# The key weights' request waits for GpSimd's constants, and the order of all engines is laid out anew

## The chip, the cores and the metric

The kernel runs on one core of a Trainium2 chip. Its engines are TensorE (PE; its weight loads are listed as PEld), VectorE (DVE), ScalarE (ACT), GpSimd (POOL) and SyncE (SP). The metric is device time in microseconds (us), the median of the runs.

## The reference

Four layers stand one behind the other on a sequence of 2048 rows of 512 numbers (bf16), and each is added to its input. Layers 1 and 3 are linear attention with 32 heads of 16 numbers, layers 2 and 4 are attention in a sliding window of 256 rows. Both kinds use one set of weights each.

```python
def _A_ref(x, wqkv, wo):                       # linear attention
    q, k, v = ...                              # x @ wqkv, by heads
    phi = lambda t: jnp.where(t > 0, t + 1, jnp.exp(t)) + 1e-6
    pq, pk = phi(q), phi(k)
    kv = jnp.einsum("bhsd,bhse->bhde", pk, v)  # sums over all rows
    z = jnp.einsum("bhsd->bhd", pk)
    num = jnp.einsum("bhqd,bhde->bhqe", pq, kv)
    den = jnp.einsum("bhqd,bhd->bhq", pq, z)[..., None] + 1e-6
    return ... num / den ... @ wo

def _B_ref(x, wqkv, wo):                       # window of W = 256 rows
    scores = jnp.einsum("bhqd,bhkd->bhqk", q, k) * (Dh ** -0.5)
    p = _softmax(jnp.where(mask, scores, -1e9))
    return ... p @ v ... @ wo

x = A_x
x = x + _A_ref(_layernorm(x), A_wqkv, A_wo)
x = x + _B_ref(_layernorm(x), B_wqkv, B_wo)
x = x + _A_ref(_layernorm(x), A_wqkv, A_wo)
x = x + _B_ref(_layernorm(x), B_wqkv, B_wo)
```

## The kernel before

The rows are cut into 16 tiles of 128, which stay in SBUF as `xres` from the first load to the last store. A tile passes through these steps. DVE takes mean and variance (line 811, 812), GpSimd the reciprocal root (814), DVE writes the normalized rows `xn` (817). They are transposed, by PE with a copy by ACT (832 and 842) for the first tiles of a layer and by a DMA that SP issues (825) for the others. PE multiplies them with the weights: line 855 makes rows by features (keys, values and the output product in the linear layers), line 867 features by rows. In a linear layer ACT takes exponentials and positive parts (876, 879), DVE joins them into `pk` or `pq` (877, 880), line 913 sums keys times values over all tiles into one PSUM bank, and line 1228 (`kvz`) closes the sums; only then can any tile's output follow (935, 944 to 947). So the first layer needs all 16 tiles' keys and values before its first output. In a window layer the scores (1004, 1052) go through ACT's exponentials (1031, 1073; 304 of them, the bulk of ACT's work), are masked by DVE (1039, 1091) and multiplied with values (1107, 1123).

Every step is recorded as a numbered operation with its engine, what it reads and what it writes. `ORDER` is a list of these numbers that a search outside of the kernel wrote: it sets in which order each engine issues its operations, which PSUM banks they take (the numbers after a colon), and which of two engines does an operation (a mark behind the number). `schedule` follows the list and only adds the waits; it moves nothing. The durations and the `land` times that stand beside operations are the search's estimates; on the chip they have no effect.

The start. GpSimd writes small constants (lines 722 to 730); DVE clears `zero` and makes the identity matrix, and later some masks. PE multiplies zeros (1265, "warm"), then branches out of that code. Each engine's first part is laid out ahead of a slow general version of the kernel, so each engine branches over that once; the operation `jump` (`warm` on PE) marks where. `loads()` issues the transfers, one behind the other on each queue: SP tile 0, 1 and 2, the value weights `w_Av`, tile 3, its branch, tile 4, the query weights `w_Aq`, and the rest; ACT the key weights `w_Ak` alone, behind its table load. ACT also fills buffers that later steps only write in part: ones in `vA` and `vt` (692), zeros in `vbd` (695, two halves), which the first window layer needs. Because `graph()` gives `deps[...] = None` for operations on one engine, that edge is an order without a wait; `True` makes a wait on a semaphore.

Of the kernel before, what the change touches and what calls it, by code (L numbers as in the profile page):

```python
# [13 lines left out]
D = 512  # L14
# [321 lines left out]
292 276:4.3.0 296:0.3 185 283 277 235 213 225:7.0 219:5.0.1 280 278 237 293 295 240 236 284' 18 19 21 279 281 220 221 262:4.4.3 263 223 222 224 238 241 264  # L336
248:6.5.0 297 266 298' 265 249 252 250 191:3.6.1 226 192 254:5.4 227' 255 195 193 197:4.5 198 256' 194 267 196 268:3.6 269 199 242 270 251 60 253 299 300:0
# [13 lines left out]
917:1 650 651 933 966 664' 1390 452 683:7.1.0 938:0.5.5 684 929 690 1387:4.0 967 473 1388 939 937 940 685' 1389' 969:0.2.1 1391 686 687 942:7 474:5.2 475 1392  # L351
943 944 970 476 661 941 971 945:0 477 946:2 947:4 1026:0.2.0 1027 1028 478:3 465:7 466 961:5.0.0 962 963 691:1 706 948 949 467 950:1 951 675:7.1 1000:2.5.2
1001 1002 994 676 677':1 964 918:4 919 973:0.2.3 920 707 1403 479:2 1404 678 680:7.3 681 1030 952:3 480:6 481 974 975 1004:0.4.5 977:3 482 982:2 682 1405
1393:3 665:7.0.1 666 953:6 2671 1406:0 972 679 954 1005 1006 976 968 692:2 667 955 724 1416 1007 1061:0.4.1 978 1062 1063 725 983 984 985:3 996:0.6.0 997 998
979 980:0 981:1 986 1407:1 693:5.2 694 1035:0.3.1 1036 708 726 701:2.2.4 1003 668 695':2 742 727:2 1417 1408:7.0.1 1409 709:1 1037 1008:0.5.3 702 698:4.0 699
# [5 lines left out]
492 493:2 1105:4.6.4 729:2.4 730 1106 1082:3 1107 731':1 1077 732 1135 1078:0.4.5 1083 734:2.2 722 740 1079 1084 1080 1109:0.6.1 1110 1111 735 1023:5 1085:1  # L361
# [4 lines left out]
765:3.0 775' 516 1092:0 1448:5 1461:7 1143 766 518 770:2.0 1134 767':0 1176 1177 1148:0.6.1 771 755:5.1.1 772' 509:1 768 769 1139 1093:4 1094 1149 1150 1095  # L366
1179:0.2.3 1157:7 1152:6 1205 1204 1180 1181 756 757 510:4 511 1147 1236:0.2.0 1151 1153 776 512 1470 528:5.15.1 529 778 1158 1154 1237 1238 532 1171:0.2.0
530 1169 779 1182 1155:0 531 1159 1160:3 1156:3 1161 1172 1127:2 780 758 1162:3 1467:4.3 1468 1210:0.5.5 1173 1211 1212 1462:7.3.3 1463 1128:3 1178 781:3
782:2 1170 1469' 759 1174 1240 777 1646:2.16.2 1213 1464 1465 1129 1130 1466 1183:0.4.2 1187:6 1188 1189 1184 1185 1190:2 1647 519:0.1 520 1191:1 1650 521 522
533 1163:3 1214:4.6.1 1648 523:2 1215 1216 1164 791:2.0.0 792 524:0 1206:0.4.0 1165 1649 1498 1499 1192:3 793 534:6.0 1186 1207 535 536 1193 537 538:0 1208  # L370
1471 1449:2.4.0 1450 1472 1239 1209 1500 1451 1194 1195:3 1245:0.6.4 783:5.1 784 1452 539:1 1196 1453 1473:1 1246 1501:0 1247 788:4.1 789 785:1 790'
1218:0.2.3 1474:6 794 525:7 526 1219 1220 786 787 1222:6 1271:0.4.1 1272 527 796 1651 1223 797 540:7 798 1224 1273 1502:15 1485 1217 799:2 1486 795 1487
# [67 lines left out]
class _Kernel:  # L440
# [816 lines left out]
    def graph(self):  # L1257
# [23 lines left out]
        for o in s.ops:  # L1281
            if o.name.startswith("fill") and "ACT" in o.engs:
                o.deps[table] = None
# [100 lines left out]
```

## Time and profile before

| | |
|---|---|
| median of three runs | 410.61 us (409.73 to 410.74) |
| profiled execution, its own time | 411.51 us |
| its span, first to last instruction | 410.1 us |
| mean granted TensorE clock | 0.996 |
| busy: PE, ACT, DVE, POOL | 386.0, 374.0, 369.2, 106.0 us |

The profile is of one execution, so its durations are held against 411.51 us. In a row of the timeline stand the start and the length in us, the engine (SPq and ACTq are what a queue issues), the line, the operation, output<-input, how many, and in brackets how long the engine had been idle before and what ended that. In rows by stretches stand the stretch, its length, and for each engine the busy time and the instructions that began in it, then the granted clock (1.00 is full), the mean busy share of the DMA engines and GB/s. Matmuls overlap in the pipeline: each is listed with its whole length, but the next begins after some 0.2 us.

### The profile page before, as it was taken

How to read it: one execution, taken by the hardware profiler on the slowest of the kernel's cores; microseconds unless marked ns; L12 is line 12 of the kernel's file. 1: busy time of each engine (PE TensorE's matmuls, PEld its weight loads, DVE VectorE, ACT ScalarE, POOL GpSimd, SP SyncE). 2: the span in 40 equal slices, each digit the busy share in tenths (PEclk: the TensorE clock that was granted, in tenths of full speed). 3: DMA queues.
4: the chain of work that ended last, by engine and by line, in shares of the span. 5: the costliest groups of instructions: out<-in, count | busy, mean ns of one | idle time of the engine just before them, and what ended most of it. 6: DMA issues, size and time to landing. Idle time of an engine off the chain costs nothing.

```text
span 410.1 us, 19106 instructions
## 1 busy us (share of the span) xinstructions
PE 386.0 (94%) x8451; PEld 276.9 (68%) x8536; DVE 369.2 (90%) x976; ACT 374.0 (91%) x484; POOL 106.0 (26%) x204
## 2 busy tenths in 40 slices
PE   7999999999999999999999999999999999989988
PEld 2545876766676767677677578676676766866766
DVE  5998999999899999999888799999999999978773
ACT  4888879999999999999999468999999999999995
POOL 2430034443151311322202101340614320414200
PEclk9999999999999999999999999999999999999998
DMA  8547435425242225122115101342433441422312
GB/s 270 144 92 204 70 62 123 65 53 85 54 80 33 57 27 86 38 45 65 42 38 73 29 2 40 76 74 42 90 72 70 63 98 29 83 60 70 64 42 81
DMA packets 77354, 29.65 MB, mean 72 GB/s; under 512 B 66896, under 2 KB 75216, under 8 KB 77264
## 3 DMA queue, kind: packets, MB, share of 16 engines
q1 hardware_dynamic: 72496, 23.28, 28.1%
q0 software_dynamic: 4096, 4.46, 6.1%
q8 instruction: 70, 1.15, 1.2%
q10 hardware_dynamic: 672, 0.59, 0.5%
q14 instruction: 20, 0.16, 0.2%
HBM read 6.29 MB, written 2.10 MB: 20 GB/s over the span
## 4 chain that ended last, share of the span: by engine, by line
PE 41%; ACT 40%; DVE 14%; DMA 2%; issue 2%; POOL 0%; SPq 0%; DVEq 0%
ACT pF L1073 30%; PE ps L855 18%; PE ps L867 9%; ACT pH L1031 8%; PE ps L1052 4%; PE ps L1123 4%; PE ps L1107 2%; DVE o L947 2%; PE ps L1004 1%; DMA xres<-in_A_x_dram 1%; DVE stats L811 1%; DVE dn L946 1%; DVE xres L890 1%; DVE pH L1039 1%; DMA xTa<-xn 1%
## 5 line engine op out<-in xcount | busy, mean ns | idle before, releaser
L1073 ACT ACTIVATE pF<-ps 128x1024 bf16<-128x1024 f32 x240 | 230.5, 1111 | 2.4 <-PE ps L1052 1.1
L814 POOL TENSOR_TENSOR rstd<-mv,const 128x1 f32<-128x1 f32 x64 | 39.0, 615 | 201.4 <-DVE mv L812 193.0
L978 POOL DMA_DIRECT2D vbd<-vt x128 | 66.9, 530 | 75.8 <-DVE vt L842 40.0
L1031 ACT ACTIVATE pH<-ps 128x1024 bf16<-128x1024 f32 (+1 forms) x64 | 60.7, 1035 | 2.7 <-PE ps L1004 2.2
L1123 PE MATMUL ps<-vbd,pF 128*128 128x34 bf16 x1856 | 60.1, 178 | 0.0
L1123 PEld LDWEIGHTS ps<-vbd,pF 128*128 128x128 bf16 x1856 | 53.7, 96 | 6.7 <-ACT pH L1031 0.2
L1052 PE MATMUL ps<-qT,kbd 32*128 32x128 bf16 x1920 | 49.0, 216 | 4.4 <-ACT pF L1073 1.6
L1091 DVE TENSOR_TENSOR pF<-pF,const 128x512 bf16<-128x512 bf16 (+2 forms) x116 | 46.4, 412 | 4.5 <-ACT pF L1073 4.3
L876 ACT ACTIVATE E<-ps 128x512 bf16<-128x512 f32 x64 | 40.2, 640 | 8.0 <-PE ps L855 4.5
L811 DVE BATCH_NORM_STATS2 stats<-xres 128x6 f32<-128x512 bf16 x64 | 43.0, 682 | 3.0 <-DMA xres<-in_A_x_dram 2.5
L1052 PEld LDWEIGHTS ps<-qT,kbd 32*128 32x128 bf16 x1920 | 28.6, 92 | 22.8 <-ACT pF L1073 10.0
L1039 DVE TENSOR_TENSOR pH<-pH,const 128x1024 bf16<-128x1024 bf16 (+1 forms) x64 | 40.9, 644 | 0.2 <-ACT pH L1031 0.2
L867 PE MATMUL ps<-xT,w_Bk 128*128 128x128 bf16 x512 | 35.3, 219 | 0.5 <-ACT vt L842 0.2
L867 PE MATMUL ps<-xT,w_Bq 128*128 128x128 bf16 x512 | 35.1, 219 | 0.1
L867 PE MATMUL ps<-xTa,w_Aq 128*128 128x128 bf16 x512 | 34.1, 219 | 0.2
L855 PE MATMUL ps<-w_Bv,xT 128*128 128x512 bf16 (+2 forms) x123 | 29.8, 350 | 3.5 <-issue 1.5
L855 PE MATMUL ps<-w_Av,xTa 128*128 128x512 bf16 (+2 forms) x132 | 32.0, 360 | 0.9 <-issue 0.5
L867 PEld LDWEIGHTS ps<-xT,w_Bq 128*128 128x128 bf16 x512 | 29.6, 98 | 4.7 <-issue 1.0
L867 PEld LDWEIGHTS ps<-xTa,w_Aq 128*128 128x128 bf16 x512 | 29.9, 98 | 3.9 <-ACT pH L1031 0.7
L855 PE MATMUL ps<-w_Ak,xTa 128*128 128x512 bf16 (+2 forms) x118 | 30.6, 373 | 1.9 <-issue 0.5
L867 PEld LDWEIGHTS ps<-xT,w_Bk 128*128 128x128 bf16 x512 | 29.4, 98 | 4.4 <-issue 2.0
L855 PE MATMUL ps<-w_Bo,oT 128*128 128x512 bf16 (+2 forms) x129 | 29.9, 342 | 2.5 <-issue 1.9
(97 smaller groups left out, 582.4 us busy)
## 6 DMA issues: line engine op xcount, KB each, us to landing
vbd<-vt POOLq DMA_DIRECT2D x128, 34.0 KB, 2.2
xres<-in_A_x_dram SPq DMA_DIRECT2D x16, 128.0 KB, 5.3
out_dram<-xres SPq DMA_DIRECT2D x15, 128.0 KB, 2.3
oT<-o SPq DMA_TRANSPOSE x60, 2.9
w_Ak<-in_A_wqkv_dram ACTq DMA_DIRECT2D x1, 512.0 KB, 5.4
w_Av<-in_A_wqkv_dram SPq DMA_DIRECT2D x1, 512.0 KB, 6.3
w_Aq<-in_A_wqkv_dram SPq DMA_DIRECT2D x1, 512.0 KB, 6.9
w_Ao<-in_A_wo_dram SPq DMA_DIRECT2D x1, 512.0 KB, 4.0
```

What stands on the lines that cost most here:

```text
L811: s.op(n + ".st", {"DVE": 0.595}, lambda e, en: e.bn_stats(st0, x.h[:]), reads=[x], writes=[st])
L814: s.op(n + ".rs", {"POOL": 0.53}, lambda e, en: e.tensor_tensor(a_rs, v, self.half.h[:], ALU.pow), reads=[mv, self.half], writes=[rs])
L855: i = e.matmul(g.h[:, a:b], xT.h[:, kt, :], w.h[:, kt, a:b], start=(kt == 0), stop=(kt == 3), skip_group_check=True)
L867: i = e.matmul(g.h[:, f * P:(f + 1) * P], w.h[:, kt, f * P:(f + 1) * P], xT.h[:, kt, :], start=(f == 0 and kt == 0), stop=(kt == 3), skip_ ...
L876: s.op(n + ".e", {"ACT": _act_cost(512)}, lambda e, en: e.activation(E.h[:], g.h, ACT.Exp, bias=0.0), reads=[g], writes=[E])
L978: return [e.dma_start(vbd.h[64 * a:64 * a + 64, j, a], vt.h[64 * j:64 * j + 64, a]) for j in range(2)]
L1031: return e.activation(d, c, ACT.Exp, bias=0.0, scale=DH ** -0.5)
L1039: return e.tensor_tensor(v, v, tr, ALU.mult)
L1052: i = e.matmul(ss[r // 2].h[:, r % 2, k * P:k * P + P], kbds[fj[m] // 2].h[32 * r:32 * r + 32, f, fj[m] % 2, :], qT.h[32 * r:32 * r + 32, ...
L1073: s.op("e%d%d" % (u, g), {"ACT": _act_cost(1024)}, lambda e, en, S=ss[g], pb=pb, g=g: e.activation(pb.h[:, 2 * g:2 * g + 2, :], S.h, ACT.E ...
L1091: return e.tensor_tensor(v, v, tr, ALU.mult)
L1123: i = e.matmul(U.h[:, c:c + 34], pFs[at[f, m][0]].h[:, r, at[f, m][1] * P:at[f, m][1] * P + P], vbds[fj[m] // 2].h[:, fj[m] % 2, :, 4 * f ...
```

## The change

The request for the key weights, ACT's first DMA, gets a wait: for every operation called `const` on GpSimd (six: the three index patterns, and the constants -0.5, 1 and 2^-9; the two `consteps`, which clear `stats`, have another name, but stand on the same engine). Seven of the search's landing times are moved, by 0.05 to 0.3. And `ORDER` is a new list.

```diff
@@ loads()
         xload(0, 2.2)
-        wload("Ak", "ACT", D, 2 * D, 4.2)
-        xload(1, 4.6)
-        xload(2, 6.0)
-        wload("Av", "SP", 2 * D, 3 * D, 7.5)
-        xload(3, 7.9)
+        wload("Ak", "ACT", D, 2 * D, 4.45)
+        xload(1, 4.3)
+        xload(2, 6.1)
+        wload("Av", "SP", 2 * D, 3 * D, 7.6)
+        xload(3, 8.0)
         late = 1.6
-        xload(4, 8.3 - late)
-        wload("Aq", "SP", 0, D, 9.8 - late)
+        xload(4, 8.35 - late)
+        wload("Aq", "SP", 0, D, 9.85 - late)
@@ graph()
         loads["ACT"][0].deps[table] = None
         for o in s.ops:
+            if o.name == "const" and "POOL" in o.engs:
+                loads["ACT"][0].deps[o] = True
             if o.name.startswith("fill") and "ACT" in o.engs:
                 o.deps[table] = None
@@ ORDER
-68 1 4 6 3 0 38 40 41 42 43 67 7 5 8 9 10 11 69 70 2 71 62:7 44 72:0 84 85 12 73:6.0 63 13 14 15 86 39 87:1 74 75:7.0.0 76 35 45 46 88:6.1 89 99 100 114 115
+38 40 41 6 7 8 42 68 43 1 2 0 9 5 3 4 10 11 69 70 71 72:0 12 84 85 13 14 86 15 62:7 99 67 44 45 46 47 48 49 50 51 73:6.0 100 39 63 87:1 37 35 74 75:7.0.0 27
...
```

All 2717 operations stay. Eleven change their engine: in the first layer three copies of values to `vA` go from DVE to ACT and two from ACT to DVE; in the first window layer one copy each way; of the copies for layer 3's keys and values one goes to ACT and one to DVE; in the last tile two copies of 128 columns go from DVE to ACT. Of PE's 962 operations 255 have another place, most of them in the first layer and at the passages into layer 2, into layer 3 and into layer 4; elsewhere neighbours swap.

ACT from its start, before. `xTa_48` and `xTa_49` are the transposed tiles 0 and 1, `E` and `pk` belong to keys:

```order
L1275 ACT_TABLE_LOAD [waits barrier_Pool_Activation_PE_DVE_SP_release]
L771 DMA w_Ak_136<-in_A_wqkv_dram 128x4x512
L842 ACTIVATE xTa_48<-ps 128x512 [waits s_PE]
L692 ACTIVATE vA_122<-const_7 128x256
L842 ACTIVATE xTa_49<-ps 128x512 [waits s_PE]
L879 ACTIVATE pk_68<-ps 128x512
L876 ACTIVATE E_64<-ps 128x512
L842 ACTIVATE vA_122<-ps 128x32x16 [waits s_PE]
L876 ACTIVATE E_65<-ps 128x512 [waits s_PE]
L879 ACTIVATE pk_69<-ps 128x512
L842 ACTIVATE xTa_51<-ps 128x512 [waits s_PE]
```

And now:

```order
L1275 ACT_TABLE_LOAD [waits barrier_Pool_Activation_PE_DVE_SP_release]
L771 DMA w_Ak_136<-in_A_wqkv_dram 128x4x512 [waits s_POOL]
L695 ACTIVATE vbd_132<-const_12 128x1632 [waits s_DVE]
L692 ACTIVATE vA_122<-const_7 128x256
L842 ACTIVATE xTa_48<-ps 128x512 [waits s_PE]
L876 ACTIVATE E_64<-ps 128x512 [waits s_PE]
L842 ACTIVATE xTa_49<-ps 128x512 [waits s_PE]
L879 ACTIVATE pk_68<-ps 128x512
L695 ACTIVATE vbd_132<-const_12 128x1632
L876 ACTIVATE E_65<-ps 128x512 [waits s_PE]
L842 ACTIVATE xTa_51<-ps 128x512 [waits s_PE]
```

The request has its wait, both clearings of `vbd` come here from the first layer's end (they stood behind some 60 operations of ACT), and the first copy of values has left this piece.

PE behind its warm-up, before (`s_dma` names are semaphores of loads):

```order
L1265 MATMUL ps<-const 128x384 x2
L855 MATMUL ps<-w_Ak,xTa 128x512 [waits s_ACT,s_dma6]
L855 MATMUL ps<-w_Ak,xTa 128x512 x3
L832 MATMUL ps<-const,xn 128x128 [waits s_DVE]
L832 MATMUL ps<-const,xn 128x128 x3
L855 MATMUL ps<-w_Av,xTa 128x512 [waits s_ACT,s_dma3]
L855 MATMUL ps<-w_Av,xTa 128x512 x3
L855 MATMUL ps<-w_Av,xTa 128x512 [waits s_ACT]
L855 MATMUL ps<-w_Av,xTa 128x512 x3
L855 MATMUL ps<-w_Ak,xTa 128x512 x4
```

And now:

```order
L1265 MATMUL ps<-const 128x384 x2
L855 MATMUL ps<-w_Ak,xTa 128x512 [waits s_ACT,s_dma13]
L855 MATMUL ps<-w_Ak,xTa 128x512 x3
L855 MATMUL ps<-w_Av,xTa 128x512 [waits s_dma3]
L855 MATMUL ps<-w_Av,xTa 128x512
L832 MATMUL ps<-const,xn 128x128 [waits s_DVE]
L832 MATMUL ps<-const,xn 128x128 x3
L855 MATMUL ps<-w_Av,xTa 128x512 x2
L855 MATMUL ps<-w_Av,xTa 128x512 [waits s_ACT]
L855 MATMUL ps<-w_Av,xTa 128x512
```

Two of tile 0's value products stand ahead of tile 1's transposes (832) now.

DVE where the first layer's sums are closed, before:

```order
L1228 TENSOR_TENSOR kvz<-ps,const 128x136 [waits s_PE]
L1228 TENSOR_TENSOR kvz<-ps,const 128x136 x3
L716 TENSOR_SCALAR const<-const 128x2x32
L716 TENSOR_SCALAR const<-const 128x2x32 [waits s_DVE]
L944 TENSOR_SCALAR dn<-ps 128x32 [waits s_PE]
L946 RECIPROCAL dn<-dn 128x32 [waits s_DVE]
```

And now:

```order
L1228 TENSOR_TENSOR kvz<-ps,const 128x136 [waits s_PE]
L1228 TENSOR_TENSOR kvz<-ps,const 128x136 x3
L944 TENSOR_SCALAR dn<-ps 128x32 [waits s_PE]
L946 RECIPROCAL dn<-dn 128x32 [waits s_DVE]
L944 TENSOR_SCALAR dn<-ps 128x32 [waits s_PE]
```

The last two constants of the key masks have left this place; the first denominator (944) follows the sums at once. SP's queue is the same up to its branch and through tile 11's load; behind that some transposes and loads change places.

More of the change, by code (lines that the diff above doesn't have):

```diff
@@ L366 @@
[L366 to L369, printed above, removed]
@@ new lines @@
+1471 780 1237 1238 1170 1171:0.2.4 1159 1160:2 1156:2 1161 1162:2 532 1467:4.1 1468 530 1172 1210:0.5.2 1178 1173 518 1211 1182 531 781:1 1462:7.2.1 1174
+1469' 1463 782:2 1212 1464 1646:3.16.3 1128:2 1129 1130 1183:0.5.1 1465 533 1466 1187:4 1188 1189 1647 1184 1185 519:0.1 520 1190:3 1472 758 1163:2 1191:1 521
+1186 522 1648 1650 1214:4.6.3 523:3 1164 1215 791:3.0.3 792 1216 1165 1498 793 1206:0.4.4 1213 1192:2 1207 534:6.0 535 1208 1193 536 1499 1449:3.4.2 1450 537
+538:0 1194 1240 1245:0.6.5 1451 1209 1195:2 1196 1452 783:5.1 784 1453 776 1246 1247 788:4.1 789 777 1218:0.2.0 1217 759 785:1 790' 1649 786 1500 794 795
@@ new lines @@
+2306:0.2.2 2307 1831 2250:0 2251 1762:0 2261 2150 1959:5.2 1960 2274:0.6.3 2308 2151 1954:4.4 2275 2276 1955 1961' 1962:5.0.5 1947 1948 1963 2297 2273 2269
+1964 1772:0.1 1773 2298:2.6.5 1956':0 1774 2299 1775 1776:1 1957 2278:4 2279 2280 1958 2300 2252:1 2302:0.2.0 1980:5.1.4 1787:6.3 1788 2303 2281:2 2282:0 2304
+2006:1 2277 1981 1789 1972:4.5 1763:1 1764 1790 1791:3 1982 2296 2216:3 2184 2329:2.6.1 1973 1765 2305 1974':1 2309 2330 1975 2301 2253:5 2254 2255 2342:0.2.1
+2331 2314:4 2283:7 2284 2285 2343 2344 2021 2007:4 2334:0.5.4 2315 2335 2286:0 2316 1777:2 2336 2287 2345 1988:0 2152 1792:0 1983 1965 1984 2217:7 2333
@@ new lines @@
+2310:0.2.3 1816 2022 2218 1966 2311 2317:1 2318:2 1977:6.3 2312 1989:0 2219 1978 2288:1 2220 1979' 2338:0.4.5 1976 1778:7 1779 1793:6 2332 2339 2365:0.2.2
+2340 1794 1990:5.0 1991 2366 2337 1780 2039 1795 2367 2313 1802:0.2 1803 2319:4 2341 2378:2.6.0 1992:2 2320 2256 2379 2380 1804 1805 1995:5.0 1996 1806:1
+1807:3 2346:0.2.2 2347 2348 1993 2057 2321 1997' 1998:7.2.2 1999 2370:0.5.3 2040 2322:3 1994 2058 2323 2371 2372 2350:4 2351 2352 2000' 2023 2024:2 2368
+2374:0.2.4 2013:7.1 1817:5.0 1818 2353:1 2349 2014 2381 2375 2376 2354:3 1819 2041 1820 1821:0 2008:4.1 1832:0.2 1833 1834 1835 2009 2010':0 1836:1 2025:1
@@ new lines @@
+2015 2324:2 2414:2.5.5 2415 2416 1808:7 1809 2001 2355:4 2373 2401:0.2.0 2402 2403 2369 1810 2356 2016:5.1.0 2017 2382:0.6.1 2357 1822:0 1823:3 1824 2404
+2018' 2358:3 2002 2359 2383 2384 2377 2059 2406:0.4.2 2407 2408 2405 1825 2011 2386:2 2387 2388 2389:1 2012 2410:0.6.3 2385 2411 2390:2 2031:3.2 2032 2412
+2042:3 2391:2 1837:3 2033' 2437:0.4.1 1838:3 1839 2438 2439 2392 2450:0.6.4 2075 2076 2393 2026:5.2 2027 2360:0 2451 2452 2093 2413 1840 2417 2394:0
+2418:0.3.0 2419 2043:2 2395 2409 2422:2 2028':1 2029 2030 2440 2423 2420 2424 2442:6.0.1 2441 2425:2 2077 2443 2019 2020 2325:5 2326 2426:0 2327 2094 2095
@@ new lines @@
+2111 2444 2052:4.0.1 2446:2.6.2 2396:3 2053 2447 2448 2361:5 2362 2486:0.2.3 2445 2054' 2078:1 2363 2049:4.3 2050 2487 2488 2427:5 2473:0.6.2 2474 2475 2051'
+2428 2421 2044:4.3 2429 2060:0 2478:0.2.5 2449 2112 2045 2430:3 2431 2453 2479 2480 2046':2 2034:7.2.3 2476 2047 2035 2454:0.5.0 2113 2055 2455 2364 2458:4
+2459 2460 2482:0.2.1 2036' 2096:2 2461:1 2079:3 2456 2462:1 2483 2085:7.0 2086 2061:0 2328 2477 2484 2067:6.1 2048 2509:0.4.0 2087' 2097:4 2510 2511 2068
+2062:7.4 2063 2522:0.2.2 2457 2069' 2463:6 2523 2524 2464 2465 2490:0.4.4 2064':0 2065 2512 2466:0 2467 2489 2432:2 2485 2114:3 2088:7.1.5 2037 2056 2089 2491
```

88 lines of the change are left out of this document (39 added, 49 removed), and 86 rows, old and new, of the table ORDER.

## The prediction

> **What bounds the kernel now.** I read the page first, then busy time by stretches of 10 us, then the timeline of the first 15 us, because the one wait that the change adds stands there. From the page the two rows on engines and on the chain that ended last; from the stretches one row for each kind of stage:
>
> ```profile
> PE 386.0 (94%) x8451; PEld 276.9 (68%) x8536; DVE 369.2 (90%) x976; ACT 374.0 (91%) x484; POOL 106.0 (26%) x204
> ...
> PE 41%; ACT 40%; DVE 14%; DMA 2%; issue 2%; POOL 0%; SPq 0%; DVEq 0%
> ...
> core 0: us, PE busy (x) PEld busy (x) DVE busy (x) ACT busy (x) POOL busy (x), PEclk, DMA share, GB/s
> 0.00:10.00 10.00, 7.04 (x30) 2.66 (x31) 5.32 (x17) 3.99 (x5) 2.45 (x15) 1.00 0.84 268
> 10.00:20.00 10.00, 9.95 (x85) 6.00 (x85) 9.85 (x32) 9.22 (x19) 3.81 (x8) 1.00 0.63 157
> ...
> 40.00:50.00 10.00, 9.92 (x186) 8.28 (x186) 8.92 (x29) 8.39 (x13) 0.00 (x0) 1.00 0.53 94
> ...
> 70.00:80.00 10.00, 9.39 (x211) 7.10 (x212) 9.70 (x26) 10.00 (x13) 3.22 (x6) 1.00 0.43 70
> ...
> 230.00:240.00 10.00, 9.87 (x52) 4.52 (x50) 7.90 (x18) 6.28 (x13) 0.79 (x2) 1.00 0.06 13
> ...
> 350.00:360.00 10.00, 9.42 (x273) 7.58 (x273) 9.05 (x24) 10.00 (x13) 3.47 (x7) 1.00 0.43 80
> ```
>
> So four stages take turns: PE is full in 10 to 50 and again near 230, ACT with its exponentials near 70 and 350. A microsecond won at the start is a microsecond at the end only if the full engine of each later stage starts earlier too. The first ten microseconds are where time is plainly lost: PE stands idle for 3.0 of them. Their timeline:
>
> ```profile
> 0.74 1.35 SPq L771 DMA_DIRECT2D xres<-in_A_x_dram  x3
> ...
> 0.79 0.45 ACTq L771 DMA_DIRECT2D w_Ak<-in_A_wqkv_dram  x1
> ...
> 1.32 0.13 POOL L724 IOTA const<- 128x8 int32 x1
> ...
> 2.13 0.43 SPq L771 DMA_DIRECT2D w_Av<-in_A_wqkv_dram  x1
> ...
> 4.60 0.41 DVE L817 TENSOR_SCALAR xn<-xres,mv,rstd 128x512 bf16<-128x512 bf16 x1 [0.68 <-POOL rstd L814]
> ...
> 6.23 0.40 PE L832 MATMUL ps<-const,xn 128*128 128x128 bf16 x4 [1.11 <-issue]
> ...
> 6.55 0.69 DVE L811 BATCH_NORM_STATS2 stats<-xres 128x6 f32<-128x512 bf16 x1 [1.54 <-DMA xres<-in_A_x_dram]
> 6.67 0.60 ACT L842 ACTIVATE xTa<-ps 128x512 bf16<-128x512 bf16 x1 [4.63 <-PE ps L832]
> 7.16 1.28 ACT L692 ACTIVATE vA<-const 128x256 bf16<-128x256 f32 x1
> ...
> 7.41 1.02 PE L855 MATMUL ps<-w_Ak,xTa 128*128 128x512 bf16 x4 [0.45 <-ACT xTa L842]
> ...
> 8.63 0.40 PE L832 MATMUL ps<-const,xn 128*128 128x128 bf16 x4 [0.20 <-DVE xn L817]
> ...
> 8.86 1.89 PE L855 MATMUL ps<-w_Av,xTa 128*128 128x512 bf16 x8
> 9.06 0.60 ACT L842 ACTIVATE xTa<-ps 128x512 bf16<-128x512 bf16 x1 [0.63 <-PE ps L832]
> ...
> w_Ak<-in_A_wqkv_dram ACTq DMA_DIRECT2D x1, 512.0 KB, 5.4
> w_Av<-in_A_wqkv_dram SPq DMA_DIRECT2D x1, 512.0 KB, 6.3
> ```
>
> Read it as three threads. PE: tile 0's normalized rows are ready at 4.60 + 0.41 = 5.01, yet its transposes start at 6.23 after 1.11 us that no engine explains ("issue"). They stand right behind PE's branch out of its warm-up code. ACT copies them out (6.67), and the key product starts at 7.41. DVE: tile 1's rows were asked for by SP's second request and let DVE wait 1.54 us, to 6.55. Loads: the key weights, asked for at 0.79, land at 0.79 + 5.4 = 6.2, and the value weights at 2.13 + 6.3 = 8.4.
>
> **The change part by part.** The durations are those of the profiled execution: 411.51 us, of which the span is 410.1. That is 0.9 us above the median of the runs, 410.61; I put the sum onto the median.
>
> *The wait.* The last of GpSimd's constants ends at 1.32 + 0.13 = 1.45. GpSimd does the same ten small instructions in another order, so ACT's request goes out near 1.5 instead of 0.79, 0.7 later. On ACT's queue the clearing of `vbd`, the spread of ones and tile 0's copy stand behind it; ACT loads its table until 6.67 - 4.63 = 2.04 anyhow, so they lose nothing. If the transfer takes 5.4 again, the key weights land at 6.9. They are read at 7.41, so the cover is 0.5 us: cost 0. If it took as long as the value weights' 6.3, they would land at 7.8, and the cost would be 0.4.
>
> *What goes first instead.* In this stretch one queue runs at a time; what the DMA queues moved from 3.0 to 4.2 us, and the rates of two stretches beside it:
>
> ```profile
> q10 hardware_dynamic: 401, 0.41, 99.2%
> q8 instruction: 1, 0.02, 5.1%
> ...
> 2.00:3.00 1.00, 1.00 (x4) 0.43 (x3) 0.07 (x1) 0.03 (x1) 0.00 (x0) 1.00 0.78 166
> 3.00:4.00 1.00, 1.00 (x4) 0.33 (x3) 0.82 (x2) 0.00 (x0) 0.00 (x0) 1.00 1.06 357
> ```
>
> q10 is ACT's queue. SP's second and third requests were out by then and moved nothing: the key weights are served whole, in the order of the requests. With the new wait tile 1's rows stand ahead of them, and DVE's 1.54 us wait goes. The Trainium skill, "DMA: Bandwidth & Descriptors", section "Queues, rings and completion order", says that each DMA engine takes turns between the queues that have work, packet by packet. The row disagrees: 401 packets of one queue, none of SP's. By that rule the delayed key weights would share with tile 2's rows and the value weights and land later than 6.9.
>
> What is late next is the value weights. The new PE order puts their first two products ahead of tile 1's transposes. They can't start before 8.4. Two products take 2 x 0.216 = 0.43 (eight take 1.89, the last of which drains 0.38: 1.51 / 7), so the transposes come at 8.9 instead of 8.63, and ACT's copy of them 0.3 later than 9.06. Meanwhile PE has only two more products to do. So I take **+0.3** for the start. Ends: -0.2 (the value weights come earlier, and PE's 0.20 before 8.63 goes) and +1.0 (SP's loads slip by the whole 0.7 as well).
>
> *Clearing `vbd` early.* It was done at 40.9 and 47.7 us, and now the first half comes right after the key weights' request, the second behind tile 0's key outputs:
>
> ```profile
> L695 ACT ACTIVATE vbd<-const x2: 1553/1556/1558, 40.9 to 47.7; 128x1632 f32<-128x1632 f32 x2
> ```
>
> The first 1.56 us and the spread (1.28, which also comes ahead of tile 0's copy) fit into ACT's idle 4.63. The second falls into 10 to 20, where ACT has 10 - 9.22 = 0.78 idle; the copies of values that move back make room. Cost 0, at most 1.56 - 0.78 = +0.8. What ACT wins in 40 to 50 is worth nothing: PE is at 9.92 there and ACT at 8.39. Without that cover it would be worth up to 3.1.
>
> *Two key-mask constants* leave the handover from the sums to tile outputs on DVE:
>
> ```profile
> 42.55 0.76 PE L935 MATMUL ps<-kvz,pq 128*128 128x136 bf16 x10
> 42.60 0.54 DVE L716 TENSOR_SCALAR const<-const 128x64 bf16<-128x64 f32 x2
> ...
> 43.11 0.19 DVE L944 TENSOR_SCALAR dn<-ps 128x32 f32<-128x32 f32 x1
> ```
>
> DVE reads PE's products at 43.11. PE starts them only at 42.55 and the first tile's last one is the sixth of ten, so DVE could read near 43.0: **-0.1** (-0.5, all of it, to 0). The constants go where DVE has room, earlier.
>
> *Copies that change engine.* Eleven. Eight are swaps within a PE-bound stretch, or cancel, and two stand at the tail. One counts: a copy of values goes from DVE to ACT inside an ACT-bound stage, where a copy costs ACT 0.62:
>
> ```profile
> 136.06 0.69 DVE L842 CAST vA<-ps 128x512 bf16<-128x512 f32 x1
> ...
> 137.40 1.94 ACT L1073 ACTIVATE pF<-ps 128x1024 bf16<-128x1024 f32 x2 [0.52 <-PE ps L1052]
> ...
> L842 ACT ACTIVATE vA<-ps 128x512 bf16<-128x512 f32 x18 | 10.7, 618 | 5.3 <-PE ps L855 5.3
> ```
>
> It now stands right ahead of those exponentials, so it fills the 0.52 that ACT waits there, and DVE is 0.69 ahead: **-0.3** (from -0.6 to +0.6). The two small ones at the tail go from DVE to ACT: 0, +-0.2.
>
> *The rest of the order.* Near neighbours swap places on PE and DVE, the work is the same. What they can change are ACT's short waits for scores in its own stages:
>
> ```profile
> ACT pH L1031 <- PE ps L1004: 2.2, 5, 0.6
> ACT pF L1073 <- PE ps L1052: 1.1, 4, 0.5
> ```
>
> 3.3 us in nine waits. A third of it either way is the bound, +-1.1; nothing in this trace says which, so 0.
>
> Sum: +0.3 - 0.1 - 0.3 = -0.1, so 410.61 becomes **410.5**. I take 0.3% of the time, 1.23 us, as what a measurement of this kernel tells from no change; -0.1 is far inside it.
>
> **Rivals.**
>
> *PE's code comes sooner (faster).* The 1.11 us before 6.23 may be the fetch of PE's code: one instruction packet stands among the key weights' in the rows above. The Trainium skill, "Runtime: NRT & Kernel Launch", section "Instruction fetch mechanics", says that a branch out of the code at hand makes the engine wait for a DMA of the target page; the trace agrees, as one such packet stands in that row. With the key weights out of its way PE could go on near 5.1. Then the key product waits for the weights alone, at 6.9: -0.5. The hole from 2 to 3 us (166 GB/s instead of 357, so 1 - 166/357 = 0.53 us of transfers) is filled and the value weights come at 7.9. With the two gains it is -0.5 - 0.1 - 0.3 = -0.9, and ACT's short waits have to give only 0.5 of their 3.3: -1.4, 409.2. Against it: the value weights still gate PE's second step. Chance 0.24.
>
> *The second clearing blocks ACT (slower).* ACT works without a break through 10 to 20, and tile 2's copy, which PE needs, stands behind the clearing. With no room made, all of 1.56 is on PE's path: +1.56 + 0.3 - 0.1 - 0.3 = +1.46, 412.1. It decides once ACT is 1.3 us late at tile 2's copy. For it speaks 9.22 of 10 busy; against it that the spread, 1.28, has left just ahead of it. Chance 0.18.
>
> *The wait does nothing.* If the queues share after all (the rule of the Trainium skill, "DMA: Bandwidth & Descriptors", above), tile 1's rows come no sooner and the key weights at 7.8: +0.4 + 0.3 - 0.1 - 0.3 = +0.3, 410.9. Same verdict as the forecast, and counted with it.
>
> **How the numbers follow.** Forecast with its like: 0.58 (409.4 to 411.8). Faster by over 0.3%: 0.24. Slower: 0.18. The range from 408.9 to 411.9 leaves out the far half of the slower case (0.1) and what would be better still than the faster one (0.1).
>
> **What would show it.** After the change: the key weights' request near 1.5; DVE's wait for tile 1's rows under 0.5; PE's transposes of tile 0 still near 6.2 (5.1 speaks for the first rival); the value weights read at 8.4 to 8.5, and tile 1's transposes at 8.9; ACT's copy of tile 2 near 12.8 (14.1 or later speaks for the second); PE full from 10 us on. Wrong would be: all loads landing half a microsecond off either way, or ACT's waits for scores adding up to 2 us or less, or 5 and more.

## The result: slower, and the profile after

| | before | after |
|---|---|---|
| median of 22 runs each, side by side | 411.41 us | 412.94 us |
| ratio, with its 95% interval | | 1.0052 (1.003 to 1.0074) |
| profiled execution, its own time | 411.51 us | 411.53 us |
| its span | 410.1 us | 410.0 us |

The kernel became 0.5% slower, 1.5 us by the medians and 2.1 by the ratio, and 412.94 lies outside of the range from 408.9 to 411.9. It is 2.4 us above the 410.5 of the forecast; 0.8 of this is the base, as before stands at 411.41 here and not at the 410.61 from which the sum started. That the two profiled executions are equal has a cause: in the one of before, PE ran its last stage at half clock for 3.41 us (from 403.81 to 407.22), and it needed 6.7 us from the start of the last exponential to the end; after needed 5.3. Below, "at full clock" stands for the mean of those executions whose mean granted clock is given as 1.00.

The page of after, its rows on engines, on the chain that ended last, and three groups (busy us and mean ns of one, then the idle time ahead of them and what ended most of it); behind them the last group in before:

```profile
PE 385.7 (94%) x8453; PEld 276.4 (67%) x8536; DVE 369.5 (90%) x973; ACT 375.7 (92%) x487; POOL 108.4 (26%) x204
...
ACT 55%; PE 34%; DVE 6%; DMA 3%; issue 2%; SPq 0%; DVEq 0%
...
L1073 ACT ACTIVATE pF<-ps 128x1024 bf16<-128x1024 f32 x240 | 230.6, 1108 | 3.4 <-PE ps L1052 2.8
...
L1031 ACT ACTIVATE pH<-ps 128x1024 bf16<-128x1024 f32 (+1 forms) x64 | 60.7, 1030 | 3.3 <-PE ps L1004 3.0
L1123 PE MATMUL ps<-vbd,pF 128*128 128x34 bf16 x1856 | 60.9, 178 | 1.0 <-issue 1.0
```

```profile
L1123 PE MATMUL ps<-vbd,pF 128*128 128x34 bf16 x1856 | 60.1, 178 | 0.0
```

The work is the same within 2.4 us for each engine. What differs is waiting: ACT waits 2.8 + 3.0 = 5.8 us for scores where it waited 3.3, and the last row has a wait of PE for nothing ("issue") in a group that had none. Two stretches of 10 us, as before in busy time by engine (PE first):

```profile
0.00:10.00 10.00, 7.99 (x30) 3.08 (x31) 6.39 (x22) 6.20 (x8) 2.88 (x16) 1.00 0.81 260
...
40.00:50.00 10.00, 9.71 (x186) 8.28 (x185) 8.60 (x27) 5.94 (x12) 0.00 (x0) 1.00 0.27 66
```

PE is busier at the start (7.99 instead of 7.04), in part because its ten warm-up matmuls take 4.45 us instead of 3.92, and has a hole at 40 to 50 (9.71 instead of 9.92). The timeline of the start, in the rows that answer to those of before, and behind them the loads (us from request to landing):

```profile
1.49 0.47 ACTq L771 DMA_DIRECT2D w_Ak<-in_A_wqkv_dram  x1
...
5.07 0.68 DVE L811 BATCH_NORM_STATS2 stats<-xres 128x6 f32<-128x512 bf16 x1
...
5.44 0.63 PE L832 MATMUL ps<-const,xn 128*128 128x128 bf16 x4
...
6.11 0.60 ACT L842 ACTIVATE xTa<-ps 128x512 bf16<-128x512 bf16 x1 [1.33 <-PE ps L832]
...
6.85 1.02 PE L855 MATMUL ps<-w_Ak,xTa 128*128 128x512 bf16 x4 [0.28 <-ACT xTa L842]
...
8.15 0.60 PE L855 MATMUL ps<-w_Av,xTa 128*128 128x512 bf16 x2 [0.28 <-DMA w_Av<-in_A_wqkv_dram]
...
8.60 0.39 PE L832 MATMUL ps<-const,xn 128*128 128x128 bf16 x4
...
9.67 0.61 PE L855 MATMUL ps<-w_Av,xTa 128*128 128x512 bf16 x2 [0.26 <-ACT xTa L842]
...
9.99 1.56 ACT L695 ACTIVATE vbd<-const 128x1632 f32<-128x1632 f32 x1
...
11.94 0.60 ACT L842 ACTIVATE xTa<-ps 128x512 bf16<-128x512 bf16 x1
```

```profile
w_Ak<-in_A_wqkv_dram ACTq DMA_DIRECT2D x1, 512.0 KB, 5.1
w_Av<-in_A_wqkv_dram SPq DMA_DIRECT2D x1, 512.0 KB, 6.0
```

The wait did what it was to do, and more: the request goes out at 1.49, DVE's wait for tile 1 is gone (5.07, no bracket), and PE goes on 0.8 us sooner (5.44 instead of 6.23). In before its first transposes came 1.47 us after its first packet of code had moved (3.79 to 4.76), and in the other four kernels without the wait 1.47 to 1.58 after; in after that packet moved from 2.48 to 3.49. But PE then waits for tile 0's copy (6.85), the value weights (8.15) and tile 1's copy (9.67). From 3.0 to 4.2 us both queues now moved packets:

```profile
q10 hardware_dynamic: 163, 0.17, 54.0%
q1 hardware_dynamic: 46, 0.05, 13.4%
```

The other end of the loss is in layer 4. PE at 313 us, in the middle of a group of equal matmuls:

```profile
313.28 0.47 PE L1123 MATMUL ps<-vbd,pF 128*128 128x34 bf16 x12
314.72 0.67 PE L1123 MATMUL ps<-vbd,pF 128*128 128x34 bf16 x20 [0.97 <-issue]
```

In the trace one matmul begins at 313.567 and the next weight load at 314.713, 1.15 us later, with no semaphore between them. ACT's scores come 0.88 us late behind it. Where the kernels stand against before, from one profiled execution of each (us; the sums are closed where the first `kvz` starts, layer 2 is full at the exponential with number 4, and the exponentials of the window layers are counted from 0):

| | first sums closed | layer 2 full | layer 3's sums | first exp. of layer 4 | 160th | 200th | 220th | 280th |
|---|---|---|---|---|---|---|---|---|
| before | 41.76 | 64.13 | 243.42 | 257.74 | 266.65 | 306.48 | 326.42 | 381.92 |
| after | +0.16 | +0.43 | -0.08 | +0.57 | +0.28 | +0.32 | +1.35 | +1.40 |
| e1 old order, wait | -0.29 | -0.27 | -0.33 | -0.33 | -0.33 | -0.33 | -0.33 | -0.19 |
| e2 new order, no wait | +0.67 | +0.94 | +0.28 | +0.94 | +0.66 | +0.71 | +2.02 | +2.08 |
| e3 new until 76 us | +0.45 | +0.73 | +0.92 | +0.92 | +0.92 | +0.92 | +0.92 | +1.58 |
| e4 new from 275 us | +0.07 | +0.08 | -0.25 | -0.25 | -0.25 | +0.11 | +0.09 | +0.15 |
| e5 new, code moved 1/2 | +0.64 | +0.91 | +0.18 | +0.83 | +0.55 | +0.60 | +0.69 | +0.75 |
| e6 old, code moved 1/2 | +1.41 | +1.49 | +0.95 | +0.95 | +0.95 | +0.95 | +1.00 | +1.00 |
| e7 new until 275 us | +0.46 | +0.74 | +0.47 | +1.13 | +0.85 | +0.92 | +2.53 | +2.57 |
| e8 new until 240 us | +0.91 | +1.19 | +1.63 | +1.60 | +1.60 | +1.61 | +4.15 | +4.17 |
| e9 new, four places back, moved 1/2 | +0.26 | +0.40 | -0.30 | -0.02 | -0.04 | +0.02 | +0.14 | +0.19 |
| e10 old, wait, moved 1/2 | -0.21 | -0.09 | -0.70 | -0.70 | -0.69 | -0.69 | -0.70 | -0.69 |
| e11 new, code moved 1/4 | +5.07 | +5.34 | +4.65 | +5.31 | +5.02 | +5.42 | +5.80 | +5.93 |
| e12 old, wait, moved 3/4 | +2.88 | +2.89 | +2.20 | +2.20 | +2.20 | +2.38 | +3.25 | +3.26 |
| e13 old, code moved 1/4 | +6.65 | +6.66 | +6.07 | +6.07 | +6.07 | +6.08 | +6.31 | +6.66 |

Of after's +1.4 us, 1.0 comes between the 200th and the 220th exponential, and 0.36 between layer 3's sums and the 160th, where layer 4 starts. What layer 2 started late is gone at layer 3's sums (-0.08). That need not be the new order's doing: e4, e6, e10 and e12, with the old order there, gained 0.33 to 0.69 on before in the same stretch, in which before has a pause of PE itself (0.38 us at 212); e1, with a pause of 0.66 us at 115, gained 0.06. In e6 and e13 the start holds a stretch at half clock too (7.61 to 11.02, and 9.65 to 16.47).

### The profile page after: what moved, and what is told of

Read it like the earlier page. It is cut to its first block, busy times and chain, and to the rows that moved or that the text cites. A ratio compares the mean times of both kernels' runs of the same rounds, so it can differ in the third digit from the quotient of the medians.

```text
span 410.0 us, 19109 instructions
## 1 busy us (share of the span) xinstructions
PE 385.7 (94%) x8453; PEld 276.4 (67%) x8536; DVE 369.5 (90%) x973; ACT 375.7 (92%) x487; POOL 108.4 (26%) x204
## 3 DMA queue, kind: packets, MB, share of 16 engines
q8 instruction: 70, 1.15, 1.1%
## 4 chain that ended last, share of the span: by engine, by line
ACT 55%; PE 34%; DVE 6%; DMA 3%; issue 2%; SPq 0%; DVEq 0%
ACT pF L1073 39%; PE ps L855 14%; ACT pH L1031 11%; PE ps L867 8%; PE ps L1123 3%; PE ps L1052 3%; ACT E L876 2%; PE ps L1107 2%; DMA w_Av<-in_A_wqkv_dram 1%; PE ps L1004 1%; ACT vA L842 1%; ACT pq L879 1%; DMA xT<-xn 1%; DVE o L947 1%; PE ps L935 1%
## 5 line engine op out<-in xcount | busy, mean ns | idle before, releaser
L814 POOL TENSOR_TENSOR rstd<-mv,const 128x1 f32<-128x1 f32 x64 | 41.6, 658 | 210.1 <-DVE mv L812 205.4
L855 PE MATMUL ps<-w_Ao,oT 128*128 128x512 bf16 (+2 forms) x125 | 28.8, 347 | 3.5 <-issue 1.9
```

The source lines that it names most:

```text
L814: s.op(n + ".rs", {"POOL": 0.53}, lambda e, en: e.tensor_tensor(a_rs, v, self.half.h[:], ALU.pow), reads=[mv, self.half], writes=[rs])
L855: i = e.matmul(g.h[:, a:b], xT.h[:, kt, :], w.h[:, kt, a:b], start=(kt == 0), stop=(kt == 3), skip_group_check=True)
```

## The experiments

Theory 1: the new order costs the time, at two passages and in layer 4. Theory 2: the wait does. Later theory A: the pause at 314 us is a late packet of PE's own code, and depends on where the code lies.

### The wait alone, and the order alone

```diff
 e1: the old ORDER, and in graph()
+            if o.name == "const" and "POOL" in o.engs:
+                loads["ACT"][0].deps[o] = True
 e2: the new ORDER, and in graph()
-            if o.name == "const" and "POOL" in o.engs:
-                loads["ACT"][0].deps[o] = True
```

> The order of before, with the key weights' wait added and nothing else. Theory 1 (the new order costs the time, most of it in layer 4: a pause of PE of 1.15 us at 314 us and 0.6 us at the passage into layer 4): no loss, 410.5 to 411.7 beside a before near 411.4, ratio 0.998 to 1.001; the key weights asked for near 1.5 us, PE going on near 5.1 us, and the exponentials of layer 4 no more than 0.3 us from before's. Theory 2 (the wait reorders the loads and costs the time): slower by 1.2 to 1.6 us, ratio 1.003 to 1.004. Theory 3 (the start's other phase lets more periods of half clock fall on PE): the granted clock is below 1 more often than before's, with the body at full clock unchanged.

> The order of the changed kernel, without the wait. Theory 1 (the order): as slow as the changed kernel, ratio 1.003 to 1.006; the last exponential about 1.3 us later than before's, with PE's pause in layer 4 if that pause belongs to the order. Theory 2 (the wait): as before, ratio 0.999 to 1.001. If the pause of PE at 314 us is a matter of chance, it is missing here and the last exponential is only 0.3 to 0.5 us late.

Measured: e1 410.79 against 410.04, ratio 1.001 (0.9982 to 1.0038), at full clock 409.93 against 410.02. e2 414.49, ratio 1.0093 (1.0059 to 1.0128), above the 1.003 to 1.006 that I had expected; its one execution at full clock took 412.21. In e1 the wait alone costs nothing, the new order without it is slower. PE's first transposes and its key product in the timelines of e1, then of e2:

```profile
5.25 0.40 PE L832 MATMUL ps<-const,xn 128*128 128x128 bf16 x4 [0.26 <-DVE xn L817]
...
7.01 1.04 PE L855 MATMUL ps<-w_Ak,xTa 128*128 128x512 bf16 x4 [1.03 <-DMA w_Ak<-in_A_wqkv_dram]
```

```profile
6.21 0.56 PE L832 MATMUL ps<-const,xn 128*128 128x128 bf16 x4 [0.57 <-issue]
...
7.55 1.02 PE L855 MATMUL ps<-w_Ak,xTa 128*128 128x512 bf16 x4 [0.45 <-ACT xTa L842]
```

With the wait PE's first packet of code starts at 2.2 to 2.9 us in all ten traces that have it, without it at 3.7 to 4.1 in all five, and the transposes follow at 5.1 to 5.4 instead of 6.2 to 6.6. At the first sums that is worth 0.29 (e1) and 0.21 (e10) in the old order, where the key weights come in time (e12 below is the exception). The pause at 314 us is in e2 too, 1.41 us long, so I took it for a part of the new order. That was wrong.

### Halves of the two orders

The list of one kernel up to an operation, then what is left in the order of the other; PSUM banks of the second part are renamed so that both fit. In short:

```diff
-ORDER = new
+e3: new[:570], rest as in old (about 76 us)
+e4: old[:1902], rest as in new, no wait (about 275 us)
+e7: new[:1902], rest as in old
+e8: new[:1650], rest as in old (about 240 us)
```

> The changed kernel (wait and new order) up to about 76 us, that is the first layer and the passage into layer 2; the order of before from there on. Theory 1 (the loss sits in layer 4): as before within 0.5 us, ratio 0.999 to 1.001; layer 2's full stage starts 0.3 to 0.5 us late, and layer 3's sums close where they did (the 0.4 us are given back). Theory 2 (the start costs it): slower by 1.2 to 1.6 us, ratio 1.003 to 1.004.

> The order of before without the wait up to about 275 us, the new order from there on (layer 4's stage and the tail). Theory 1 with the loss in the stage of layer 4: slower by 0.9 to 1.2 us, ratio 1.002 to 1.003, with PE's pause near 314 us. If the loss is the passage into layer 4 (238 to 275 us), which keeps the old order here: as before. Theory 2 (start): as before, ratio 0.999 to 1.001.

> The changed kernel up to about 275 us (start, passage into layer 2, layers 2 and 3, passage into layer 4), the order of before from there on. Theory 1 (passages and a late packet): the passage into layer 4 costs 0.6 us from the closing of layer 3's sums to the first exponential of layer 4, 0.4 after the stage has filled; no pause of PE at 314 us; the last exponential 0.3 to 0.6 us later than before's; at full clock 410.4 to 410.8. Theory 2 (the stage of layer 4 itself has the worse order): as before, 410.0.

> The changed kernel up to about 240 us (start, passage into layer 2, layers 2 and 3's keys and values), the order of before from there on. Theory 1: layer 2's full stage starts 0.4 to 0.9 us late, layer 3's sums give most of it back (-0.1 to +0.3 against before), the passage into layer 4 costs nothing, and at full clock the time is 409.9 to 410.4. If the start were what costs the time: 411.2 to 411.9 at full clock.

Measured, ratio and time at full clock beside before's: e3 1.0064 (1.0042 to 1.0086), 411.98 to 410.02; e4 1.0019 (1.0001 to 1.0037), 410.85 to 410.02; e7 1.0016 (0.9991 to 1.0041), 411.79 to 410.62; e8 1.0025 (0.9992 to 1.0059), 410.63 in two executions. e3 is beyond what either theory gave, e7 a microsecond above its 410.4 to 410.8. e4's loss of 0.8 at full clock is not in its profiled execution (+0.15 at the 280th), and e8's two executions at full clock are level with before though its profiled one is 4.17 behind. So one trace doesn't stand for every execution of its kernel, and whether a pause comes in each of them isn't shown.

Two terms are steady. From the first sums to the full stage of layer 2 every kernel with the new order there loses 0.27 or 0.28 (after, e2, e3, e5, e7, e8), those with the old order 0.00 to 0.12. From layer 3's sums to the 160th exponential the new order loses 0.36 to 0.38 (after, e2, e5, e7), the old one 0.03 or less. PE at the two places, of before and then of after (layer 4 behind the dots):

```profile
55.02 0.61 PE L867 MATMUL ps<-xT,w_Bq 128*128 128x128 bf16 x8
55.47 0.59 PE L855 MATMUL ps<-w_Bv,xT 128*128 128x512 bf16 x2
...
56.88 0.30 PE L1004 MATMUL ps<-qT,kbd 32*128 32x64 bf16 x16
...
254.20 1.06 PE L867 MATMUL ps<-xT,w_Bk 128*128 128x128 bf16 x16
...
257.38 0.29 PE L1004 MATMUL ps<-qT,kbd 32*128 32x64 bf16 x16
```

```profile
55.13 0.59 PE L855 MATMUL ps<-w_Bv,xT 128*128 128x512 bf16 x2
55.56 1.06 PE L867 MATMUL ps<-xT,w_Bq 128*128 128x128 bf16 x16
56.45 0.60 PE L855 MATMUL ps<-w_Bv,xT 128*128 128x512 bf16 x3
57.39 0.30 PE L1004 MATMUL ps<-qT,kbd 32*128 32x64 bf16 x16 [0.34 <-ACT qT L842]
...
254.34 0.59 PE L855 MATMUL ps<-w_Bv,xT 128*128 128x512 bf16 x2
254.77 1.06 PE L867 MATMUL ps<-xT,w_Bk 128*128 128x128 bf16 x16
...
257.95 0.29 PE L1004 MATMUL ps<-qT,kbd 32*128 32x64 bf16 x16
```

In after a value product stands ahead of the query product (layer 2) or of the key product (layer 4), and the first scores, on which the exponentials wait, come later. How much of it is due to that product, e9 tests below.

The pause at 314 us didn't follow the halves. e4 has the new order there and no pause at that place; e7 (1.76 us) and e8 (1.46) have the old order there and a pause, against what I expected of both. e3 has a step of its own at 79 us, a seam: where the two lists meet, ACT waits 0.59 for scores. That is why it is still 0.92 behind at layer 3's sums. The rest of its 1.58 comes with two pauses of PE, 0.59 us at 339.6 and 0.34 at 368.7, where it has the old order.

### Where PE's code lies

PE's instructions come in packets of 16 KB (70 packets on the queue "q8 instruction" in both kernels). In the traces of after, e2, e7 and e8 the pause stands ahead of the same recorded PE instruction, the 12,318th, and pauses elsewhere stand close to whole multiples of 255 from it (16 times less 2 in before at 212 us, 34 times less 11 in e8 at 117 and less 12 in e1 at 115; some records are missing from a trace). The pauses of e3 (above) and one of 0.35 us in e4 at 277 are within 3 of such a multiple. Before, e1 and e3 have the old order there, so it has late packets too. In after no such packet moved from 309.4 to 312.0 us, then one did; the DMA queues in the two stretches:

```profile
q1 hardware_dynamic: 685, 0.26, 40.2%
q0 software_dynamic: 71, 0.08, 20.3%
```

```profile
q1 hardware_dynamic: 437, 0.12, 74.4%
q0 software_dynamic: 45, 0.06, 70.9%
q8 instruction: 1, 0.02, 5.9%
```

The edit, abridged, adds code that is never executed, to the version that PE branches over, and so moves all that lies behind it:

```diff
                 nc.sync.wait_ge(done.sem, done.val)
+                [nc.tensor.matmul(ps[:, 0, 0:1], zero, zero[:, 0:1]) for _ in range(64)]
                 gen.put(gen.order)
```

e5 puts this into the changed kernel and e6 into the one before; e11 and e13 do the same with 32, a quarter of a packet.

> The changed kernel; the only edit is that the slow general version, which PE branches over, gets 64 more one-column matmuls (128 instructions with their weight loads), so that all of PE's later code lies half a 16 KB packet further on. Nothing more is executed. Theory A (PE's pause of 1.15 us at 314 us is a late packet of its own code, held up behind the transposes): the packet falls due at another moment, the pause is gone there, the exponentials between the 200th and the 220th lose no more than 0.2 us against before (1.0 in the changed kernel), and at full clock the time is 0.8 to 1.2 us less than the changed kernel's 411.96, unless another packet is late. Theory B (the pause belongs to the order of PE and DVE): it stays, and so does the time, 411.5 to 412.3 at full clock.

> The kernel before with the same 64 matmuls in the version that is branched over. Theory A (packets of code that come late make pauses wherever they meet the transposes): the packets fall due elsewhere, some pause of 0.3 to 1.2 us may come or go, and the time at full clock moves by -0.4 to +1.2 us from before's 410.0. Theory B (where code lies makes no difference): 409.8 to 410.2 at full clock.

> The changed kernel with PE's later code moved by a quarter of a packet (32 one-column matmuls with their weight loads in the version that is branched over). Theory A (late packets of code): the page of code that was late at 314 us begins some 1 to 1.5 us earlier; either it is in time and the time at full clock is near that of the half packet, 0.6 to 0.9 above before, or another one is late by 0.3 to 1.8 us at a multiple of 256 instructions from it, never inside a packet. Theory B (the order makes the pause): the pause stays at the same matmul of the same operation.

> The kernel before with PE's later code moved by a quarter of a packet. In the changed kernel this put a boundary between the third and the fourth transposing matmul of tile 0, where PE then stood for 4.2 us while the weights were loading. Theory A (where the code lies decides, whatever the order): the same here, PE stands for 3.5 to 5.5 us in tile 0's transposes, the first sums close 4 to 6 us late, ratio 1.010 to 1.018. Theory B (the new order or the wait brings the pause): as before, ratio 0.998 to 1.002.

Measured: e5 1.0023 (1.0001 to 1.0044), 411.35 at full clock beside 410.62; e6 0.9983 (0.9963 to 1.0002), 410.21 beside 410.62; e11 417.93, ratio **1.0171** (1.0132 to 1.0209); e13 417.53, ratio **1.0183** (1.0154 to 1.0213). In e5 the pause is gone and no other at a boundary is as long as 0.25 us: the 220th exponential is 0.09 later against before than the 200th. Its time at full clock is 0.6 below after's 411.96, less than the 0.8 to 1.2 that I expected; a gap of 0.73 us to before remains. In e11 and e13 the pause is longer than I expected (0.3 to 1.8 us in e11; in e13 the sums close 6.65 late, not 4 to 6). PE in e5, its 32 products without a break, then in e11, then in e13:

```profile
313.57 0.98 PE L1123 MATMUL ps<-vbd,pF 128*128 128x34 bf16 x32
```

```profile
5.44 0.53 PE L832 MATMUL ps<-const,xn 128*128 128x128 bf16 x3
10.15 0.27 PE L832 MATMUL ps<-const,xn 128*128 128x128 bf16 x1 [4.19 <-issue]
```

```profile
6.22 0.34 PE L832 MATMUL ps<-const,xn 128*128 128x128 bf16 x3 [0.58 <-issue]
11.76 0.26 PE L832 MATMUL ps<-const,xn 128*128 128x128 bf16 x1 [5.20 <-issue]
```

The boundary fell between the third and the fourth matmul of tile 0's transposes, and the packet moved from 7.56 to 8.68 in e11 and from 9.23 to 10.35 in e13. PE's second packet starts between 7.4 and 10.1 us in all 15 traces, so it wasn't later here: PE needed it sooner. The loads moved then too; that they hold it is likely, but not shown. Old order or new, wait or none: theory A is shown for the place. What is not shown is why the packet at 314 us came late in some kernels. It began 0.8 us after the boundary before it in before and e1, 1.4 in e3 and e4, 2.7 in after and e2, 2.9 and 3.2 in e7 and e8, while e3 and e8 had the same transfers around it. Over eight traces the share of the two busy queues just after a boundary doesn't go with the delay. That stays open.

### Four places put back, and the best pieces together

```diff
 e9: e5, and in PE's order
-81 (v0 of tile 0) 88 (transposes of tile 1)      +88 81
-557 (v0, layer 2) 554 555 (its queries)          +554 555 557
-1854 (v0, layer 4) 1847 1848 1851 1852 (its keys, queries)   +1847 1848 1851 1852 1854
-1855 (v1, layer 4) 2129 (first scores)           +2129 1855
 e10: e1 with the 64 matmuls of e6;  e12: e1 with 96
```

> The changed kernel with its later PE code half a packet further on (as in the run whose code was moved), and four of PE's operations put back: tile 1's transposes ahead of tile 0's value products; the first value product of layer 2 behind its query product; the two of layer 4 behind the query product and behind the first scores. Theory 1 (these places cost the time): from the closing of the first sums to the fourth exponential of layer 2 no more than 0.1 us is lost against before (0.27 in the changed kernel), from layer 3's sums to the 160th exponential no more than 0.15 (0.37), the first sums close 0.2 to 0.5 earlier than with the new start (41.5 to 42.2), and at full clock the time is 0.5 to 0.9 us less than with the code moved alone, that is level with before, -0.3 to +0.3. Theory 2 (the loss is spread over the new order of all engines): the two passages stay at 0.27 and 0.37 and the time at 0.7 above before's.

> The order of before with the wait, and the later PE code half a packet further on. Both edits alone were level with before (-0.1 and -0.4 us at full clock). If the two gains are real and add up: ratio 0.998 to 0.999 and 409.5 to 409.9 at full clock beside a before of 410.0 to 410.6. If the wait wins nothing in the end, as before within 0.2 us.

> The order of before with the wait, PE's later code three quarters of a packet further on (96 one-column matmuls with their weight loads in the version that is branched over). With half a packet the ratio was 0.9984. If that gain comes from the wait and the missing pauses: again 0.997 to 0.999 (409.5 to 410.0 at full clock beside a before of 410.0 to 410.6), the first sums closed 0.2 to 0.4 us before those of before. If it was luck of where the code lay: 0.999 to 1.003, with a pause of 0.3 us or more at a boundary of a packet.

Measured: e9 1.0014 (0.9989 to 1.0038), 410.65 at full clock beside 410.27; e10 0.9984 (0.9961 to 1.0008), 409.73 beside 410.27; e12 1.001 (0.9994 to 1.0026), 410.77 beside 410.11. e9 gave back only a half at the first passage (0.27 became 0.14) and a third at the second (0.37 became 0.26; at the first exponential 0.65 became 0.28), less than I expected, though the end came out level: at the 280th exponential +0.19 instead of +0.75. So the products that I had put back explain a third to a half of what the passages cost; where the rest comes from stays open. At the first passage PE then waited for something else instead:

```profile
57.34 0.30 PE L1004 MATMUL ps<-qT,kbd 32*128 32x64 bf16 x16 [0.18 <-DVE kbd L968]
```

The first sums closed at +0.26, inside the scatter of five kernels with the new start and the wait (0.16 to 0.91), so that part is not told apart. e10 is the fastest of all, but its interval holds 1; e12, the same but for a quarter of a packet, was level with before, as the theory of luck had it, and has pauses of 0.45, 0.95 and 0.44 us at boundaries (301, 318 and 387 us). No version is shown to beat before. e12 also shows what can go wrong with the wait in its profiled execution: landing time of the key weights, PE's wait, and busy time by stretches of 3.41 us (PE's is the second number, the granted clock stands ahead of the DMA share):

```profile
w_Ak<-in_A_wqkv_dram ACTq DMA_DIRECT2D x1, 512.0 KB, 7.8
```

```profile
9.37 1.89 PE L855 MATMUL ps<-w_Ak,xTa 128*128 128x512 bf16 x4 [3.18 <-DMA w_Ak<-in_A_wqkv_dram]
```

```profile
5.50:8.92 3.42, 0.69 (x7) 0.30 (x5) 2.11 (x9) 1.77 (x2) 0.87 (x2) 1.00 1.09 363
8.92:12.33 3.41, 2.96 (x11) 1.31 (x12) 1.94 (x6) 0.61 (x2) 1.00 (x3) 0.50 0.99 314
```

Behind SP's loads the key weights took 7.8 us and landed at 9.3; in eight of the other nine traces with the wait PE read them at 6.6 to 7.3 (in e11 its code came later than they did).

## Why the prediction was wrong, step by step

- **The wait**: right for after. The request went out at 1.49 (1.5 forecast), the weights landed at 1.49 + 5.1 = 6.6 (6.9), ahead of the end of tile 0's copy, cost 0. The cover was thin: in e1, e3, e5, e7 and e9 the weights landed last (6.66 to 7.26), and in e12 they cost 3.18 us.
- **What goes first instead**: wrong in its reading. I took it from one stretch that queues are served one by one, and set the rule of the Trainium skill, "DMA: Bandwidth & Descriptors", section "Queues, rings and completion order", aside. In after both queues moved packets in that stretch, as the rule says. DVE's wait went all the same: tile 1's rows had been asked for first, and landed at 4.79 instead of 6.53.
- **Transposes of tile 0 still near 6.2**: wrong, 5.44. The mechanism of the faster rival, PE's code sooner, is what happened, in all ten traces with the wait. Its price was too high: 0.2 to 0.3 us at the first sums in the old order, not 0.5, since the value weights come next.
- **The start, +0.3**: about right. The value weights were read at 8.15 (8.4 to 8.5) and tile 1's transposes came at 8.60 (8.9). At the first sums +0.16, in the five kernels with this start and the wait 0.52 in the mean. But at layer 3's sums after was level with before, so the start doesn't account for the end.
- **Second clearing**: right. ACT copied tile 2 at 11.94, before 12.8, and the slower rival's mechanism didn't occur. The slower side came by a way that no rival had.
- **Two key-mask constants, -0.1**: nothing. The first denominator is read 1.34 us after the sums, 1.35 before; DVE now waits for PE there.
- **Value copy at 136 us, -0.3**: nothing. After gains 0.17 from the 60th to the 70th exponential (0.43 to 0.26 behind before) and is at 0.45 again by the 80th.
- **Tail copies, 0**: right; at full clock 5.3 us from the last exponential in after and e4, 5.3 in e3 and 5.4 in e7 with the old tail.
- **The rest of the order, 0 with +-1.1**: this is the step that failed, in two ways. First, the sum had no term for PE's own code. In after a packet of it came late at 314 us and held PE for 1.15 us; that is 1.0 of the 1.4 us, and e5 took it away by moving code that isn't executed. I had reckoned with a wait for code at the start alone, the 1.11 us of the first rival. Second, I bounded the swaps by a third of ACT's waits in the full stages, but the order lost 0.36 us at the passage into layer 4 (and 0.27 into layer 2, which isn't told apart at the end). I had put those rows of PE's order down as neighbours that swap; the value products ahead of the scores are a third to a half of it, by e9. ACT's waits for scores came to 5.8 us, beyond the 5 that I had named as a sign of being wrong.

The profile shows 1.4 us of the median's 1.5 to 2.1. At full clock the mean of after's ten executions, 411.96, stands 1.3 to 1.9 above before's 410.02 to 410.62, so these agree. 12 of after's 22 executions had a lower mean clock than 1.00, beside 39 of 103 of before in the experiments; chance alone would give such a difference in about one case of six.

## What to carry to other kernels

A new order of a long unrolled program is also a new place of its code and of its transfers in time, and a single pause can outweigh the order: move the code by some instructions that aren't executed, in both versions, before you credit or blame an order. Look at each passage between stages for what stands ahead of the operation that the next stage's full engine waits for; inside the full stage of layer 4 the new order lost 0.1 us or less apart from the pause (0.28 to 0.32 and 1.35 to 1.40), at the passage into it 0.36. And look for "issue" waits inside groups of equal matmuls: the long ones here stood where a packet of code begins. Take more than one trace before you price such a pause.

## What the runs showed of the hardware that I had not expected

PE resumed 1.3 to 1.6 us after its packet of code had moved, in all pauses that I measured (from 313.24 to 314.71 in after, 8.68 to 10.15 in e11, 10.35 to 11.76 in e13). The Trainium skill, "Runtime: NRT & Kernel Launch", section "Instruction fetch mechanics", calls the crossing of such a boundary mostly hidden; the traces agree for most of some 70 packets, and disagree by up to 5.2 us (e13) while the first weights were loading.

Half clock can follow a pause and add to its cost. PE in e8 around the late packet, then two of its stretches of 3.41 us, laid on the change of clock at 316.11, and behind them before's stretch ahead of its half clock at 403.81:

```profile
314.44 0.45 PE L1123 MATMUL ps<-vbd,pF 128*128 128x34 bf16 x11
316.17 0.79 PE L1123 MATMUL ps<-vbd,pF 128*128 128x34 bf16 x21 [1.29 <-issue]
```

```profile
312.70:316.11 3.41, 2.19 (x91) 1.91 (x86) 2.80 (x7) 3.41 (x5) 2.26 (x5) 1.00 1.08 118
316.11:319.52 3.41, 3.13 (x45) 1.92 (x47) 1.75 (x7) 1.50 (x3) 0.63 (x1) 0.50 0.02 5
```

```profile
400.40:403.81 3.41, 3.28 (x117) 2.93 (x112) 1.59 (x5) 3.41 (x5) 0.00 (x0) 1.00 0.31 91
```

In e8's stretch with the pause PE was busy for 2.19 of 3.41 us, and the next one ran at half clock; in e12 it was 0.69. But after with its pause of 1.15 us, e2 with 1.41 and e7 with 1.76 have a mean granted clock of 1.000, and in before a stretch without such a pause, busy for 3.28 us, stands ahead of half clock. So the busy share of the stretch doesn't tell alone, and that the pause brought the half clock in e8 isn't shown. The Trainium skill, "TensorE: Matmul & The Clock Gate", Part 1, tells of a free-running window of 3413 ns after which the clock is set; the length agrees, 3413 ns or twice that for each period of half clock inside these traces. But it speaks of an idle window ahead of half clock, and the stretches shown here were busy for 20 to 96% of their time.
